# One written list of steps for attention and early routing, in place of a planner with priorities

## The chip, the cores and the metric

The program runs on one core of a Trainium2 chip. Its engines work side by side and each takes its own instructions strictly in order: TensorE (PE: matmuls and transposes into the eight PSUM banks; PEld: its weight loads), VectorE (DVE), ScalarE (ACT), GpSimd (POOL) and SyncE (SP), which only queues DMA transfers here. An instruction that waits for another engine holds up all that stands behind it on its own. The metric is the time of the whole program on the device in microseconds (us).

## What is computed

Three layers follow each other: windowed attention, a mixture of 8 experts that sends each token to one expert, and a dense layer.

```python
def _attn_ref(q, k, v):                       # (2, 8, 576, 64) each
    scores = scale * np.matmul(q, k.transpose(0, 1, 3, 2))
    mask = (rel >= 0) & (rel < 64)            # rel = row - column
    scores = np.where(mask, scores, -1000000000.0)
    attn = np.exp(scores - np.max(scores, axis=-1, keepdims=True))
    attn = attn / (np.sum(attn, axis=-1, keepdims=True) + 1e-09)
    return np.matmul(attn, v)
...
x = attn_out.transpose(0, 2, 1, 3).reshape(1152, 512)
# experts: the best of 8 by x @ w_gate, at most 288 tokens each;
# each token gets gate * (relu(x @ w1[e]) @ w2[e])    w1 (8, 512, 1024), w2 (8, 1024, 512)
# dense: h = x @ w_in; out = (h * clip(h + 3, 0, 6) / 6) @ w_out      w_in (512, 2048)
```

## The kernel before, in words

Attention goes over the 1152 tokens in nine tiles of 128 tokens with all 8 heads (j = 0 to 8); a tile has two groups g = 2j and 2j + 1. All is in float32. The steps of tile j, by the short names that the kernel gives them:

- `lq`, `lk`, `lv`: SP queues the loads of 256 KB each (L472). A load needs a free slot among 3 for q, 4 for k, 3 for v.
- `tq`, `tk`, `tv`: TensorE turns them, four transposes each (L504); `eq`, `ek`, `ev` copy the result out of PSUM, on ScalarE or VectorE (L456 to L462). `cv0`, `cv1`, `cv2` are GpSimd's copies of the values into three rotating pairs of value tiles (L486); they need the values step of three (`cv2`: two) tiles ago to be over, since it reads the tile that they overwrite. A slot for v is free when its turn and its copies are done.
- `gw`, `ew`, `tw`, `ex`: the router's product with the values (L534), its copy, a small turn (L548), and copies into columns beside the values.
- `s`: the scores of both groups, 32 small matmuls (L568). It uses one pair of banks, so the next tile's must wait until this tile's masks have read them.
- `m`: VectorE's mask with the row maximum, four pieces a group (L581). `e`: ScalarE's exponentials, four a group (L594). `pt`, `ep`: the probabilities are turned (L604) and copied out.
- `av`: the values step, 32 matmuls (L622), into the one pair of accumulator banks. `f`: VectorE's finish, which divides, adds up the router's logits (L634 to L650) and frees these banks. `st`: SP stores the tile's rows to memory (L654). In the last tile ScalarE does the division (L642).

After five tiles early routing starts: `top` chooses the expert of 640 tokens (L130 to L138), `pp` counts on TensorE, `pl`, `fl` and `gE` on VectorE pick the busiest expert and the places of its first 128 tokens, `ix` and `ie` make an index of it, and `ga` on GpSimd gathers their rows from memory by an indirect DMA (L799), `sE` scales them, `tE` turns them (L814) and `xE` copies them. `wl.u.h` are eight loads of 512 KB of that expert's weights, possible once `pl` has told which expert (L271, L274), and `e0` to `e3`, `er`, `et`, `eh` are its products for three of four units of weights. Behind the last tile `ch`, `cn`, `pL`, `rk`, `sa`, `px`, `sx` place the remaining tokens and `g0` gathers the first rows; `gt`, `hot`, `gc`, `pg`, `sg` make the gates. The rest of the experts and the dense layer follow in an order that another planner in the kernel sets; it takes over the clocks of this stage.

Each step is a node with engines and estimated costs, needs, a ring that it takes a slot of, and rings that it frees. In the kernel before, `run_nodes` (L425) plans greedily: of all nodes whose needs are met it takes the one with the smallest key, made of the time at which it could start on an engine by the planner's clocks, a priority from a table and its cost. For a copy that either engine can do, the same key picks ScalarE (A) or VectorE (V). The central lines:

```python
key = (t + EPS * prio + (c if len(engs) > 1 else min(engs.values())) * CW, prio)
able.append((key, name, e, t, c))
...
best = min(able)
```

Of the kernel before, what the change touches and what calls it, by code (L numbers as in the profile page):

```python
# [23 lines left out]
def tile_kernel(ctx, tc, q, k, v, w_gate, w1, w2, w_in, w_out, out, cap):  # L24
# [24 lines left out]
    NA = 3 * E  # L49
# [267 lines left out]
    GAP = -0.2  # L317
    EPS, CW, COLD, LAG = 0.015, 0.3, 6.0, 0.15
    PRIO = {'q': -30, 'k': -29, 'v': -27, 'tq': -7, 'eq': 8, 'tk': -10, 'ek': 3, 'cv': 1, 'tv': 1, 'ev': 2, 'gw': 1, 'ew': 1, 'tw': 1, 'ex': -4, 's': 2, 'm': 5, 'e': 2, 'pt': 2, 'ep': 9, 'av': 2, 'f': 8, 'st': 0, 'top': -5, 'tail': 2, 'ear': 78, 'hot': 60, 'gt': 25, 'fl': 13, 'ga': 58, 'xE': 5, 'turn': 20}
    CS = {'xE': 1.15, 'ep': 1.07, 'eq': 1.07, 'sE': 1.15, 'rk': 1.3, 'q': 1.15, 'v': 0.7}  # L320
    with ExitStack() as actx:
# [74 lines left out]
        nodes, done, emitted = {}, {}, []  # L396
# [3 lines left out]
        clock = dict.fromkeys(("PE", "A", "V", "P", "D"), 0.0)  # L400

        def node(name, prio, engs, fn, needs=(), take=None, free=(), lag=LAG):
            engs = {e: c * CS.get(name[0] if isinstance(name, tuple) else name, 1.0) for e, c in engs.items()}
            nodes[name] = (prio, engs, fn, needs, take, free, lag)

        def ready(name):
            _, _, _, needs, take, _, _ = nodes[name]
            r = 0.0
            for n in needs:
                if n not in done:  # L410
                    return None
                r = max(r, done[n])
            if take:
                order = taken[take]
                if len(order) >= rings[take]:
                    old = order[len(order) - rings[take]]
                    if freed.get((take, old), (0, 0.0))[0] < holders.get((take, old), 1):
                        return None
                    r = max(r, freed[take, old][1])
            return r  # L420

        holders, now = {}, [0.0]

        def run_nodes():
            while nodes:  # L425
                able = []
                for name, (prio, engs, *_) in nodes.items():
                    r = ready(name)
                    if r is None:
                        continue  # L430
                    for e, c in engs.items():
                        t = max(clock[e], r)
                        if e == "PE" and t < COLD:
                            c = 2 * c
                        key = (t + EPS * prio + (c if len(engs) > 1 else min(engs.values())) * CW, prio)
                        able.append((key, name, e, t, c))
                best = min(able)

                able = [a for a in able if a[3] + a[4] <= best[3] + GAP]
                best = min([best] + able, key=lambda a: (a is best, a[0][1])) if able else best  # L440
                _, name, e, t, c = best
                _, _, fn, _, take, free, lag = nodes.pop(name)
                if take:
                    taken[take].append(name)
                now[0] = t
                fn(e)
                clock[e] = t + c
                done[name] = t + c + lag
                for ring, owner in free:
                    n, was = freed.get((ring, owner), (0, 0.0))  # L450
                    freed[ring, owner] = n + 1, max(was, t + c + 0.1)
# [210 lines left out]
        node("wg", 6, {"D": 0.3}, lambda e: load_wg(), lag=2.0)  # L662
        node("rc", 30, {"P": 6.0}, lambda e: routing_constants())
        A_V = {"A": 0.5, "V": 0.6}
        for j in range(NJ):
            p = 10 * j + (PRIO["tail"] if j == NJ - 1 else 0)
            for nm in ("q", "k", "v"):
                node(("l" + nm, j), p + PRIO[nm], {"D": 1.25}, load_rows(nm, j), take=nm, lag=2.0)
            parts = 3 if j + 1 < NJ else 2
            holders["v", ("lv", j)] = 1 + parts  # L670
            node(("tq", j), p + PRIO["tq"], {"PE": 0.44}, turn_rows(("q", j), ("tq", j)), [("lq", j)], "t", [("q", ("lq", j))])
            node(("eq", j), p + PRIO["eq"], {"A": 0.5, "V": 0.6}, q_out(j), [("tq", j)], "qd", [("t", ("tq", j))])
            node(("tk", j), p + PRIO["tk"], {"PE": 0.44}, turn_rows(("k", j), ("tk", j)), [("lk", j)], "t", [("k", ("lk", j))])
            node(("ek", j), p + PRIO["ek"], A_V, k_out(j), [("tk", j)], None, [("t", ("tk", j))])
            for i in range(parts):
                old = j - NV + (i == 2)
                node(
                    (f"cv{i}", j), p + PRIO["cv"] + i, {"P": 0.6}, v_copy(j, i), [("lv", j)] + [("av", old)] * (old >= 0),
                    None, [("v", ("lv", j))],
                )  # L680
            node(("tv", j), p + PRIO["tv"], {"PE": 0.44}, turn_rows(("v", j), ("tv", j)), [("lv", j)], "t", [("v", ("lv", j))])
            node(("ev", j), p + PRIO["ev"], A_V, v_out(j), [("tv", j)], "vT", [("t", ("tv", j))])
            node(("gw", j), p + PRIO["gw"], {"PE": 0.27}, v_gate(j), [("ev", j), "wg"], "x", [("vT", ("ev", j))])
# [1410 lines left out]
```

## Time and profile before

| | us |
|---|---|
| median of 3 runs | 417.3 (416.82 to 417.35) |
| the profiled execution | 416.61 |
| its span, first to last instruction | 414.9 |
| TensorE busy | 400.3 (96% of the span) |
| VectorE busy | 280.1 (68%) |
| ScalarE busy | 233.9 (56%) |
| GpSimd busy | 49.3 (12%) |

Times in the trace are microseconds from the span's start. The span is shorter than the execution by what lies around it. Attention and early routing end at about 61 us; the matmuls behind them, at L244, hold the rest. Busy time of TensorE contains the latency of a matmul, so a step's price is read from its start to the next one's start.

### The profile page before, as it was taken

What the parts mean: (1) busy time and instruction counts of PE and PEld (TensorE: products, weight loads), DVE (VectorE), ACT (ScalarE), POOL (GpSimd) and SP (SyncE); (2) the same over time, 40 slices, a digit from 0 to 9 for tenths busy, and PEclk for the clock granted to TensorE, in tenths of its full rate; (3) what the DMA queues carried; (4) which work ended last, traced back from release to release, by engine and by line L of the source; (5) the groups of instructions that cost most, each with busy time, mean ns of one, the idle gap of its engine ahead of it and who ended that gap; (6) DMA issues with size and microseconds to landing.
All of it is one profiled execution on the core that took longest, in us unless ns stands there. A gap on an engine that the chain in (4) does not pass through costs nothing.

```text
span 414.9 us, 8440 instructions
## 1 busy us (share of the span) xinstructions
PE 400.3 (96%) x3066; PEld 341.7 (82%) x3066; DVE 280.1 (68%) x781; ACT 233.9 (56%) x510; POOL 49.3 (12%) x109
## 2 busy tenths in 40 slices
PE   8999889999999999999999999999999999999992
PEld 5787666668999898898989999888888888999981
DVE  1988977599789789876789999358895222322430
ACT  3886863687586747666885566267573222322330
POOL 8733402030012000000000000000000000200111
PEclk9999999999999999999999999999999999999997
DMA  9999685987787999899700560033500000100101
GB/s 168 212 217 222 218 294 171 308 285 240 228 263 226 352 300 303 286 344 346 263 2 0 165 242 0 2 101 103 203 2 2 0 0 2 74 27 2 51 28 57
DMA packets 63842, 65.43 MB, mean 158 GB/s; under 512 B 30688, under 2 KB 47072, under 8 KB 63792
## 3 DMA queue, kind: packets, MB, share of 16 engines
q1 hardware_dynamic: 62224, 59.79, 46.4%
q0 software_dynamic: 1568, 5.01, 3.6%
q8 instruction: 26, 0.43, 0.4%
q14 instruction: 24, 0.20, 0.1%
HBM read 60.08 MB, written 4.72 MB: 156 GB/s over the span
## 4 chain that ended last, share of the span: by engine, by line
PE 90%; DVE 5%; ACT 2%; issue 1%; POOL 0%; POOLq 0%; ACTq 0%; DVEq 0%
PE banks L244 76%; PE banks L504 2%; PE banks L622 2%; PE banks L568 1%; PE banks L604 1%; DVE neg L581 1%; PE banks L1475 1%; PE banks L661 1%; PE banks L1500 1%; PE banks L534 1%; PE banks L1310 1%; ACT pe L594 1%; PE banks L1559 1%; PE banks L1408 0%; DVE xt L649 0%
## 5 line engine op out<-in xcount | busy, mean ns | idle before, releaser
L244 PE MATMUL banks<-x,wt 128*128 128x320 f32 (+3 forms) x432 | 79.8, 336 | 0.0
L244 PEld LDWEIGHTS banks<-x,wt 128*128 128x128 f32 x432 | 70.8, 188 | 7.1
L244 PE MATMUL banks<-wt,g 128*128 128x512 f32 x288 | 69.6, 390 | 0.0
L263 DVE TENSOR_TENSOR wt<-raw,wt 128x512 fp32r<-128x512 f32 x100 | 64.6, 685 | 4.9 <-ACT wt L258 4.6
L1621 DVE SCALAR_TENSOR_TENSOR gf<-r,banks 128x320 f32<-128x320 f32 (+3 forms) x48 | 26.6, 553 | 60.3 <-ACT r L1618 60.1
L1618 ACT ACTIVATE r<-banks,c_three 128x320 f32<-128x320 f32 (+3 forms) x48 | 27.9, 582 | 68.4 <-PE banks L244 68.2
L244 PEld LDWEIGHTS banks<-wt,g 128*128 128x128 f32 x288 | 53.7, 188 | 10.6
L258 ACT CAST wt<-raw 128x512 fp32r<-128x512 f32 x100 | 58.7, 628 | 4.5 <-PE banks L244 4.0
L244 PE MATMUL banks<-xT,wt 128*128 128x224 f32 (+2 forms) x288 | 38.2, 282 | 0.0
L244 PE MATMUL banks<-h,wt 128*128 128x224 f32 (+2 forms) x288 | 37.0, 279 | 0.0
L244 PEld LDWEIGHTS banks<-xT,wt 128*128 128x128 f32 x288 | 34.8, 191 | 1.6 <-issue 0.4
L244 PEld LDWEIGHTS banks<-h,wt 128*128 128x128 f32 x288 | 34.6, 192 | 0.8 <-issue 0.8
L1624 ACT CAST g<-gf 128x320 fp32r<-128x320 f32 (+2 forms) x40 | 21.3, 534 | 16.4 <-DVE gf L1621 16.4
L1627 DVE TENSOR_TENSOR g<-gf,g 128x320 fp32r<-128x320 f32 (+2 forms) x40 | 23.3, 584 | 10.1 <-ACT g L1624 9.4
L1664 POOL DMA_INDIRECT out_dram<-raw,cidx x4 | 3.9, 981 | 204.5 <-DVE raw L1658 196.9
L244 PE MATMUL banks<-x,wt_fixed 128*128 128x320 f32 (+3 forms) x144 | 26.8, 337 | 0.4 <-ACT x L1391 0.4
L244 PEld LDWEIGHTS banks<-x,wt_fixed 128*128 128x128 f32 x144 | 23.5, 188 | 3.0 <-ACT x L1391 0.7
L206 ACT ACTIVATE c<-raw 128x512 f32<-128x512 f32 x32 | 21.5, 673 | 6.2 <-DVE raw L229 4.7
L244 PE MATMUL banks<-wt_fixed,g 128*128 128x512 f32 x96 | 23.2, 390 | 0.0
L222 DVE SCALAR_TENSOR_TENSOR c<-raw,c 128x512 uint32<-128x512 uint32 x32 | 22.1, 690 | 0.8
L581 DVE CUSTOM_DVE_ANT_0 neg<-banks,tmask 128x128 f32<-128x128 f32 x72 | 16.2, 286 | 9.4 <-PE banks L568 9.4
L594 ACT ACTIVATE pe<-neg,nmx 128x128 f32<-128x128 f32 x72 | 22.3, 392 | 0.1
(310 smaller groups left out, 629.4 us busy)
## 6 DMA issues: line engine op xcount, KB each, us to landing
raw<-in_moe_w_dram SPq DMA_DIRECT2D x56, 512.0 KB, 5.9
raw<-in_moe_w_in_dram SPq DMA_DIRECT2D x16, 512.0 KB, 6.6
raw<-in_moe_w_out_dram SPq DMA_DIRECT2D x16, 512.0 KB, 6.1
early<-in_moe_w_dram SPq DMA_DIRECT2D x8, 512.0 KB, 6.6
x_dram<-xt SPq DMA_DIRECT2D x9, 256.0 KB, 2.8
q_sb<-in_q_dram SPq DMA_DIRECT2D x8, 256.0 KB, 3.9
k_sb<-in_k_dram SPq DMA_DIRECT2D x8, 256.0 KB, 4.8
v_sb<-in_v_dram SPq DMA_DIRECT2D x8, 256.0 KB, 4.5
```

The source lines that it names most:

```text
L206: nc.scalar.activation(box["c"].bitcast(F32), box["hi"].bitcast(F32), AF.Abs)
L222: nc.vector.scalar_tensor_tensor(out=box["c"], in0=box["hi"], scalar=0xC0000000, in1=box["c"], op0=ALU.bitwise_and, op1=ALU.bitwise_or,)
L244: nc.tensor.matmul(out, l, r, start=(start and n == 0), stop=(stop and n == len(pairs) - 1))
L258: nc.scalar.copy(hi, r)
L263: V.tensor_tensor(out=lo, in0=r, in1=hi.bitcast(F32), op=ALU.subtract)
L504: nc.tensor.transpose(pt[:, hp, :], t[:, 2 * hp : 2 * hp + 2, :].rearrange("p h d -> p (h d)"), ident)
L581: V.tensor_tensor_reduce(out=neg[:, hp, :], in0=box["sp", g][:, hp, :], in1=tmask[:, first, :], scale=-1.0, scalar=3.0e38, op0=ALU.add, op ...
L594: nc.scalar.activation(pe[:, hp, :], neg[:, hp, :], AF.Exp, bias=nmx[:, hp : hp + 1], scale=-1.0)
L1618: nc.scalar.activation(r, ph, AF.Relu, bias=c_three)
L1621: V.scalar_tensor_tensor(out=gf, in0=r, scalar=6.0, in1=ph, op0=ALU.min, op1=ALU.mult)
L1624: nc.scalar.copy(hi, gf)
L1627: V.tensor_tensor(out=lo, in0=gf, in1=hi.bitcast(F32), op=ALU.subtract)
```

## The change

The table of priorities, the key and the choice among ready nodes go away. In their place stands a written list of all steps, `ATTENTION`, each with the engine for a copy (`:a` ScalarE, `:v` VectorE). `run_nodes` goes through it and issues step by step; each engine gets its steps in the order of the list. The clocks that it still keeps serve the planner of what follows. They start at other values, and the estimated costs of the nodes are other numbers.

```diff
+    ATTENTION = """
+        lq.0 tq.0 lk.0 tk.0 lk.1 eq.0:a lq.1 lq.2 ek.0:a tk.1 s.0 lv.0 m.0 tq.1 ek.1:a tq.2 eq.1:a m.1 e.0 wg tv.0
...
-        clock = dict.fromkeys(("PE", "A", "V", "P", "D"), 0.0)
+        clock = {"PE": 5.0, "A": 1.3, "V": 1.2, "P": 7.1, "D": 2.9}
...
         def run_nodes():
-            while nodes:
-                able = []
...
-                best = min(able)
...
+            name_of = {n if isinstance(n, str) else ".".join(map(str, n)): n for n in nodes}
+            for word in ATTENTION.split():
+                word, _, e = word.partition(":")
+                name = name_of.pop(word)
+                engs, fn, _, take, free, lag = nodes[name]
+                e = {"a": "A", "v": "V"}[e] if e else next(iter(engs))
+                t, c = max(clock[e], ready(name)), engs[e]
+                if e == "PE":
+                    if t < 7.1:
+                        c *= 1.95
+                    f = FORMS.get(word.split(".")[0], 128)
+                    if f != form[0]:
+                        form[0] = f
+                        c += 0.094
                 if take:
                     taken[take].append(name)
                 now[0] = t
                 fn(e)
                 clock[e] = t + c
-                done[name] = t + c + lag
+                done[name] = t + c + (LAG[e] if lag is None else lag)
...
-        node("ga", p + PRIO["ga"], {"P": 1.04}, early_gather, ["ie"], lag=6.0)
+        node("ga", {"P": 0.4}, early_gather, ["ie"], lag=6.0)
```

No instruction is added or taken away in sum; some copies change engine (of the copies of turned probabilities, 12 on ScalarE and 6 on VectorE, which was 14 and 4; of the other full copies more are on ScalarE). The loads stand in the order q0, k0, k1, q1, q2, v0, router weights, k2, v1 and so on, where before each tile had q, k, v in turn. TensorE's row has s.5 and s.6 ahead of the values step of tile 4; behind the routing counts stand the turn tv.5 and, further on, the last turns. On SP the load of tile 7's values stands behind those of tile 8 and needs the slot of tile 5's; behind it come the stores of tiles 4, 2, 3, 1, then six early weight loads, the store of tile 5 and two more. In the tail TensorE has pt.15, av.6, gw.8, pt.14, pt.17, tw.8, av.7, pt.16, tE between the last scores and the last values; before it had pt.15, av.7, pt.16, pt.17, tE. Behind attention it starts with three half products of the early expert before the counts, where it had two.

Three places, first as they were and then as they are (the new file's lines are a few numbers off: L655 is the old L649). VectorE from tile 3's finish on, before (`xt` and `logits` end a finish, `kT`, `vw`, `qd` are copies out of PSUM, `top_m` is the choice of experts):

```order
L650 TENSOR_REDUCE logits<-lv 128x8
L456 COPY kT<-banks 128x4x2x64
L456 COPY vw<-banks 128x128
L458 TENSOR_SCALAR qd_183<-banks 128x512
L634 TENSOR_SCALAR rd<-banks 128x8
L635 RECIPROCAL rd<-rd 128x8
L637 TENSOR_TENSOR lv<-banks,rd 128x64
L649 TENSOR_TENSOR xt<-banks,rd 128x512
L650 TENSOR_REDUCE logits<-lv 128x8
L130 TENSOR_REDUCE top_m<-logits 128x5
```

And now, from the copies ahead of tile 3's finish to the first mask piece behind it:

```order
L462 COPY pT<-banks 128x512
L462 COPY vw<-banks 128x128
L640 TENSOR_SCALAR rd<-banks 128x8
L641 RECIPROCAL rd<-rd 128x8
L643 TENSOR_TENSOR lv<-banks,rd 128x64
L655 TENSOR_TENSOR xt<-banks,rd 128x512
L656 TENSOR_REDUCE logits<-lv 128x8
L587 ISA neg,nmx<-banks,tmask 128x128
L587 ISA nmx 128x1
```

Three more pieces of this mask group follow, then the finish of tile 4 and the choice of experts. A mask group has moved ahead of the choice; two more moved ahead of it further up.

ScalarE's end of attention, before (`c` is the scaling of the gathered rows, `early` the copy of their turn):

```order
L460 COPY pT<-banks 128x512
L594 ACTIVATE pe<-neg,nmx 128x128 x8
L462 ACTIVATE c_1188<-c_1188,sgE 128x512
L460 COPY pT<-banks 128x512
L460 COPY early<-banks 128x512
```

And now:

```order
L600 ACTIVATE pe<-neg,nmx 128x128 x4
L466 COPY vw<-banks 128x128
L466 COPY pT<-banks 128x512
L600 ACTIVATE pe<-neg,nmx 128x128 x4
L466 COPY vx_187<-banks 128x8x8
L466 COPY vy_190<-banks 64x8x8
L468 ACTIVATE c_1191<-c_1191,sgE 128x512
L466 COPY pT<-banks 128x512
L466 COPY early<-banks 128x512
```

A small copy, a copy of probabilities and two pieces of router columns have come in between.

GpSimd around the gather, before (`vx`, `vy` are the value tiles, `A1t` products for the late routing, `c` the gathered rows):

```order
L486 TENSOR_SCALAR vy_189<-v_sb 64x8x64
L486 TENSOR_SCALAR vy_190<-v_sb 64x8x64
L486 TENSOR_SCALAR vx_187<-v_sb 128x8x64
L486 TENSOR_SCALAR vy_190<-v_sb 64x8x64
L891 TENSOR_TENSOR A1t<-A_93,c_tok 128x128 x5
L799 DMA c_1188<-x_dram,eI 128x512
```

And now:

```order
L492 TENSOR_SCALAR vx_186<-v_sb 128x8x64
L492 TENSOR_SCALAR vy_189<-v_sb 64x8x64
L492 TENSOR_SCALAR vx_187<-v_sb 128x8x64
L492 TENSOR_SCALAR vy_190<-v_sb 64x8x64
L800 DMA c_1191<-x_dram,eI 128x512
L892 TENSOR_TENSOR A1t<-A_93,c_tok 128x128 x2
L492 TENSOR_SCALAR vy_190<-v_sb 64x8x64
L892 TENSOR_TENSOR A1t<-A_93,c_tok 128x128 x3
```

The gather has moved ahead of the five products and of one value copy (of tile 7); the four copies in front of it are two of tile 7 and two of tile 8.

## Rows read from the trace of the kernel before

**Rows 1.** Page, chain that ended last: share of the span by engine
```profile
PE 90%; DVE 5%; ACT 2%; issue 1%; POOL 0%; POOLq 0%; ACTq 0%; DVEq 0%
```

**Rows 2.** Windows: us, PE, PEld, DVE, ACT, POOL busy, PEclk, DMA share, GB/s
```profile
20.00:25.00 5.00, 5.00 (x92) 4.03 (x91) 4.20 (x25) 4.01 (x12) 1.39 (x3) 1.00 0.81 193
...
40.00:45.00 5.00, 4.05 (x64) 2.97 (x60) 5.00 (x50) 4.66 (x15) 0.23 (x1) 1.00 0.34 74
...
50.00:55.00 5.00, 3.81 (x81) 2.84 (x79) 4.73 (x27) 3.84 (x12) 2.22 (x4) 1.00 1.07 379
```

**Rows 3.** Timeline of TensorE, one period: start us, us, instruction
```profile
21.56 0.65 PE L604 MATMUL banks<-ident,pe 128*128 128x128 f32 x4
...
23.02 1.10 PE L568 MATMUL banks<-kT,qd 64*64 64x128 f32 x32
24.06 0.66 PE L604 MATMUL banks<-ident,pe 128*128 128x128 f32 x4
24.64 0.43 PE L534 MATMUL banks<-vT,wgb 128*32 128x128 f32 x8
...
25.74 0.28 PE L622 MATMUL banks<-vy,pT 128*64 128x73 f32 x1
...
26.92 0.66 PE L604 MATMUL banks<-ident,pe 128*128 128x128 f32 x4
```

**Rows 4.** Timeline of VectorE, from the choice of experts to the last mask
```profile
38.40 0.20 DVE L130 TENSOR_REDUCE top_m<-logits 128x5 f32<-128x40 f32 x1
...
46.91 0.16 DVE L778 CAST rhsE<-et 128x5 f16<-128x5 f32 x1
...
47.38 0.60 DVE L783 TENSOR_SCALAR rhsE<-et 128x5 f16<-128x5 f32 x1
...
49.44 0.15 DVE L634 TENSOR_SCALAR rd<-banks 128x8 f32<-128x8 f32 x1
...
50.78 0.28 DVE L581 CUSTOM_DVE_ANT_0 neg<-banks,tmask 128x128 f32<-128x128 f32 x1
...
52.25 0.29 DVE L581 CUSTOM_DVE_ANT_0 neg<-banks,tmask 128x128 f32<-128x128 f32 x1
...
56.41 0.28 DVE L581 CUSTOM_DVE_ANT_0 neg<-banks,tmask 128x128 f32<-128x128 f32 x1
```

**Rows 5.** Chain in order of time, end of attention: start us, us, what
```profile
56.27 2.45 ACT pe L594 x8
58.71 0.62 ACT c L462
...
60.04 1.20 PE banks L622 x32
```

**Rows 6.** Timeline behind attention: TensorE's longest wait, the first late gather
```profile
66.69 1.13 PE L244 MATMUL banks<-early 128*128 128x256 f32 x4 [0.75 <-ACT first_w L842]
...
68.75 0.94 POOL L799 DMA_INDIRECT first_w<-x_dram,sidx  x1 [16.35 <-DVE sidx L999]
```

**Rows 7.** Page, DMA issues: tile, count, KB each, median us to landing
```profile
v_sb<-in_v_dram SPq DMA_DIRECT2D x8, 256.0 KB, 4.5
```

**Rows 8.** Groups by line, 0 to 62 us: busy us, mean ns of one
```profile
L460 ACT COPY pT<-banks 128x512 f32<-128x512 f32 x14 | 8.1, 582 | 5.4 <-PE banks L604 5.1 <-DVE nmx L581 0.3
...
L456 DVE COPY pT<-banks 128x512 f32<-128x512 f32 x4 | 2.7, 684 | 0.0
...
L456 DVE COPY vw<-banks 128x128 f32<-128x128 f32 x6 | 1.7, 290 | 0.5 <-PE banks L534 0.4
```

**Rows 9.** Timeline of GpSimd before the early gather
```profile
47.29 0.65 POOL L486 TENSOR_SCALAR vy<-v_sb 64x512 f32<-64x512 f32 x1 [7.07 <-PE banks L622]
...
51.21 1.20 POOL L799 DMA_INDIRECT c<-x_dram,eI  x1 [0.18 <-DVE nmx L581]
```

**Rows 10.** Tiles c (the early gather) and early (its expert's weights): from issue to landing
```profile
DMA to landing us min/median/max: 7.1/7.1/7.1
...
DMA to landing us min/median/max: 3.5/6.6/8.2
```

More of the change, by code (lines that the diff above doesn't have):

```diff
@@ L399, in tile_kernel, with node @@
         freed = {}
-        clock = dict.fromkeys(("PE", "A", "V", "P", "D"), 0.0)
-        def node(name, prio, engs, fn, needs=(), take=None, free=(), lag=LAG):
-            engs = {e: c * CS.get(name[0] if isinstance(name, tuple) else name, 1.0) for e, c in engs.items()}
-            nodes[name] = (prio, engs, fn, needs, take, free, lag)
+        clock = {"PE": 5.0, "A": 1.3, "V": 1.2, "P": 7.1, "D": 2.9}
+        def node(name, engs, fn, needs=(), take=None, free=(), lag=None):
+            nodes[name] = (engs, fn, needs, take, free, lag)
         def ready(name):
-            _, _, _, needs, take, _, _ = nodes[name]
+            _, _, needs, take, _, _ = nodes[name]
             r = 0.0
             for n in needs:
-                if n not in done:
-                    return None
                 r = max(r, done[n])
@@ L415, in ready @@
                 if len(order) >= rings[take]:
[L416 to L419, printed above, removed]
-            return r
-        holders, now = {}, [0.0]
+                    r = max(r, freed[take, order[len(order) - rings[take]]])
+            return r
+        now, form = [0.0], [128]
+        FORMS = {"gw": 32, "s": 64, "av": 73}
+        LAG = {"PE": 0.2, "V": 0.14, "A": 0.15, "P": 0.1, "D": 1.5}
         def run_nodes():
-            while nodes:
-                able = []
[L427 to L436, printed above, removed]
-                best = min(able)
[L439 to L442, printed above, removed]
+            name_of = {n if isinstance(n, str) else ".".join(map(str, n)): n for n in nodes}
[12 more added lines that the diff above has]
+                        c += 0.094
                 if take:
@@ L677, in tile_kernel @@
                 node(
[L678 removed]
+                    (f"cv{i}", j), {"P": 0.6}, v_copy(j, i), [("lv", j)] + [("av", old)] * (old >= 0),
                     None, [("v", ("lv", j))],
                 )
[L681 to L682 removed]
@@ L702, in tile_kernel @@
                 needs += [("ex", j - 1), ("cv2", j - 1)]
[L703 removed]
+            node(("av", j), {"PE": 1.1}, values(j), needs, "o", free)
             if j + 1 < NJ:
[L705 to L711 removed]
+                node(("f", j), {"V": 1.35}, lambda e, j=j: finish(j), [("av", j)], "xt", [("o", ("av", j))])
+                node(("st", j), {"D": 0.75}, lambda e, j=j: store_x(j), [("f", j)], None, [("xt", ("f", j))])
+            else:
+                node(("f", j), {"V": 1.0}, lambda e, j=j: finish(j), [("av", j)])
         A1E = ac.tile([128, NE, 128], F16, name="A1E")
```

138 lines of the change are left out of this document (70 added, 68 removed).

## The prediction, made before the changed kernel ran

> **What bounds the kernel now.** I read the chain of waits first: 90% of the span is TensorE, so the kernel as a whole is bound by the matrix engine, and VectorE has 5% [rows 1]. Next the windows of five microseconds, to see where TensorE is short of work: it is busy 5.00 of 5.00 us from 20 to 25, but 4.05 from 40 to 45, 3.81 from 50 to 55 [rows 2]. So attention falls in two parts. In the first, the timeline of TensorE shows a period of 5.36 us for a tile of 128 tokens (the same transposes start at 21.56 and at 26.92) with nothing idle between; a new order can gain nothing there, it can only lose. In that period a score step (L568) takes 1.04 us, a router step, a turn and the small turn behind it 1.10 together, and the 32 matmuls with the values 1.18 [rows 3]. In the second part VectorE is the limit: it is busy 5.00 of 5.00 us from 40 to 45 and 4.73 from 50 to 55 [rows 2]. There it has the early routing between the mask steps: from the choice of experts at 38.40 until the last mask (56.41 + 0.28 = 56.70) it works with hardly a gap for 18.3 us [rows 4]. The last piece is ScalarE's: the chain goes from the masks to eight exponentials (56.27 to 58.71), the scaling of the gathered rows, the turn of these and, at 60.04, the last matmuls with the values [rows 5]. Whatever brings these forward brings everything behind them forward, since TensorE has little idle time after it: the largest left is 0.75 us at 66.69 [rows 6].
>
> **The change part by part.** I sum from one event to the next, in the profiled execution's own time (416.61 us, of which 414.9 are the span; 0.7 below the median of 417.30). The difference is then taken from the median.
>
> *Up to the finish of tile 4.* The new row of TensorE has, before the values step of tile 4, two score steps more and one v turn, one router step and one small turn less: 2 x 1.04 - 1.10 = +1.0 us [rows 3]. Its kinds of steps are the same and the number of changes between them nearly so, so while TensorE is full, the finish of tile 4 comes 1.0 us later: VectorE's choice of experts starts at 38.40 + 1.0 = 39.4. The start of the kernel bounds this from both sides. The new load order asks for tile 0's values sixth instead of third, and a load of values takes 4.5 us from issue to landing [rows 7], several under way at once; a turn that waits for one may wait about a microsecond (an estimate: the period of 5.36 us covers three loads and a store, so a load each 1.2 us or so). Against that, fewer turns wait there for a ScalarE copy. I take 0, with +-1.0 for the range.
>
> *VectorE from the choice to the last mask.* The order shows the same instructions there except for these, which the new order leaves out of the stretch: three mask groups of four pieces, now ahead of tile 4's finish; one finish of a tile, now behind the masks; two copies of turned probabilities and one small router copy, now on ScalarE. Prices: eight mask pieces start from 50.78 to 52.25, 0.21 each, so 12 x 0.21 = 2.5; a finish from 49.44 to 50.78, 1.3; the copies 2 x 0.68 + 0.29 = 1.65, of which the end overlaps the next instruction, so 1.5 [rows 4, 8]. Together 5.3 us of 18.3; 13.0 stay. The last mask ends at 39.4 + 13.0 = 52.4 instead of 56.7. The one before it ends 0.84 sooner, at 51.6.
>
> *ScalarE's tail.* What went off VectorE comes back here, and this is the cost of the change. Behind the masks the old row has two exponential steps (2.45), the scaling (0.62) and one copy. The new row has: exponentials 1.22, a small copy 0.29, a copy 0.58, exponentials 1.22, two pieces of the router columns (0.4, an estimate from the 0.29 of the small copy, which VectorE needs), the scaling 0.62, a copy 0.58, and about 0.2 until the matmuls start [rows 5, 8]: 5.1 us. From 51.6 that ends at 56.7. But a copy stands ahead of these exponentials that needs a turn which TensorE does behind the last score step; I put 0.6 for that, which makes 57.3. A second way to the same matmuls agrees: the accumulator bank. Tile 6's finish follows the last mask (52.4 + 1.3 = 53.7), then tile 7's values (1.18, + 0.3 for two hand-overs), then its finish 1.3 and 0.2: 56.7 if nothing else is late. I take 57.3 against 60.0 before: **-2.7 us**.
>
> *The gather.* On GpSimd it now stands behind four value copies, two of them of tile 7. That tile's load is queued on the load queue behind one that needs tile 4's value step, and its slot comes free with a turn that stands behind the routing counts. Step by step: choice 39.4 + 1.3, counts and turn 1.0 (41.7), load 4.5 (46.2), four copies at 0.65 (48.8), gather 7.1 from issue to landing (55.9) [rows 7, 9, 10]. From landing to the last values the new ScalarE row has scaling 0.62 and copy 0.58, with hand-overs 1.4: 57.3. It is just hidden, and bounds the end as much as ScalarE does. Before, it landed at 51.21 + 7.1 = 58.3, just under the exponentials that ended at 58.7, so it hid there too. Bounds by the nearest rows: the weight loads beside it landed in 3.5 to 8.2 us [rows 10], so 3.6 less, which the other two ways hide, or 1.1 more. The early weights are asked for behind that load and four stores, from about 43.5 on. The first one used is the fifth in the row; asked for some 2 us later, it is there by 54 even at 8.2, before it is needed: nothing gained or lost.
>
> *Behind attention.* The order of what follows is nearly the same. The counts for the late routing come after one more half product (about +0.9 us for VectorE's ranks), and TensorE's wait of 0.75 at 66.69 [rows 6] gets work beside it. VectorE has slack there, and all weights are asked for from the same points of the chain. I take 0, bounds -0.7 and +0.9.
>
> Sum: -2.7 us; 416.6 would become 413.9, and the median 417.3 becomes **414.6 us**.
>
> **A rule weighed.** The last routing step L783, 5 elements a row, took 0.60 us where its like L778 took 0.16; it ended at 47.98, just behind a value copy of GpSimd that ran from 47.29 to 47.94 [rows 4, 9]. The Trainium skill (SBUF — State Buffer, "SBUF: two separate sides") says that VectorE, in an instruction with two SBUF inputs or in a two-port mode, and GpSimd share a port pair as an exclusive lock, so that the loser waits for the whole instruction. By that rule, with which the trace agrees, this change can cost what rival (a) does; without it the sum stands.
>
> **The rivals.** (a) *Vector steps held by GpSimd's copies.* Before, GpSimd stood idle for 7.07 us while VectorE did the routing [rows 9], so only one copy met it. Now value copies run while the gate step is under way or just behind. If all four hold a step as the one above was held (0.45 us), VectorE's stretch grows by 1.8 us and the gain shrinks to 0.9: 416.4. For it: the row. Against: most vector steps there read PSUM or are over in 0.2 us, and all four would have to meet one. (b) *More than forecast.* The waits in the tail fall away, and TensorE is left with its own work: its idle time is 0.95 us from 40 to 45 and 1.19 from 50 to 55 [rows 2], and the chain shows TensorE out of 2.4 us while the eight exponentials run. All of it gone is 4.5 us: 412.8. Against: one accumulator bank pair and ScalarE's longer tail. (c) *Slower: the gather becomes the bound.* Behind the counts the row is serial: turn, load of tile 7's values, copies, gather, scaling, copy. It decides once the gather lands later than about 58.6, that is, when load and gather together take over 14.3 us instead of 11.6. With tile 7's load as slow as the slowest weight load, 8.2 us [rows 10], the gather lands at 41.7 + 8.2 + 2.6 + 7.1 = 59.6 and the last values start at 61.0: +1.0, 418.3. For it: TensorE's row has the turn of the gathered rows ahead of the last values, so nothing slips past it. Against: the weight loads are queued behind this load, and the gather's 7.1 was measured with them under way. (d) *The kernel's rest takes the gain back*, because the weight stream and not TensorE sets the pace behind attention: 417.2. Against it stand the chain's 90% on TensorE [rows 1] and that the loads are asked for from the same chain.
>
> **How the numbers follow.** Forecast 0.56, its own range 413.2 to 416.0 from the +-1.0 of the start and the two ends of the last part. (a) 0.14, (b) 0.14, (c) 0.10, (d) 0.06. A measurement of this kernel tells 0.2%, 0.8 us, from no change. Faster: forecast, (b), and most of (a): 0.56 + 0.14 + 0.10 = 0.80. The same: the rest of (a), (d) less a bit: 0.09. Slower: (c) and a lost start: 0.11. The range reaches into (b) below and to where (d) and the mild half of (c) lie above: 412.4 to 417.6.
>
> **What would show it.** In the new profile: TensorE full up to about 36 us; the choice of experts (L130) within 1 us of 39.4; the last mask near 52.4 with no copy of probabilities on VectorE between; ScalarE nearly without a gap from there to the last values; the gather issued near 48.8 and landed before 56; the last values near 57.3; the first gather behind attention 2 to 3 us sooner than 68.75 [rows 6]. The prediction is wrong if TensorE waits at the start for loads by more than a microsecond, if the gather is issued after 51, or if the last values come sooner and the kernel ends no sooner.

## The result, and the profile after

The changed kernel takes **413.25 us** (median of 4 runs, 412.68 to 413.33) against 417.13 us for the kernel before on the same chip (4 runs, 416.82 to 417.35): ratio 0.9905, 95% interval 0.9887 to 0.9922, so 3.9 us or 0.9% faster. Forecast were 414.6 us, with a range of 412.4 to 417.6 and a chance of 0.80 for faster. The profiled span went from 414.9 to 411.5 us, but TensorE's last matmuls start 3.92 us earlier (402.42, now 398.50): behind the last matmul, where the output is written, the second profile takes half a microsecond longer.

The chain of waits in the new profile, shares by engine, answers to [rows 1]. VectorE went from 5% to 3%, and DMA, which had no share before, now has 3%:

```profile
PE 89%; DMA 3%; DVE 3%; ACT 2%; issue 1%; POOL 0%; POOLq 0%; ACTq 0%; DVEq 0%
```

The windows answer to [rows 2] (same columns, with two more windows):

```profile
20.00:25.00 5.00, 5.00 (x94) 4.34 (x94) 4.79 (x27) 4.48 (x14) 2.44 (x4) 1.00 1.00 194
40.00:45.00 5.00, 4.84 (x88) 3.85 (x87) 5.00 (x42) 4.59 (x15) 1.20 (x2) 1.00 0.86 253
45.00:50.00 5.00, 4.14 (x74) 3.02 (x69) 4.88 (x34) 4.94 (x16) 3.21 (x5) 1.00 0.96 339
50.00:55.00 5.00, 4.82 (x89) 3.98 (x87) 4.05 (x25) 4.52 (x16) 0.00 (x0) 1.00 1.08 368
55.00:60.00 5.00, 3.88 (x47) 3.30 (x46) 2.62 (x11) 2.90 (x9) 1.73 (x4) 1.00 0.93 340
```

From 40 to 45 TensorE has 4.84 us of work instead of 4.05, from 50 to 55 it has 4.82 instead of 3.81. VectorE is still nearly full from 40 to 50 (5.00 and 4.88); ScalarE now is too, up to 55 (4.59, 4.94 and 4.52). What is left idle on TensorE lies mostly from 45 to 50 (0.86 us) and from 55 to 60 (1.12).

VectorE's timeline answers to [rows 4] (start, us, engine, line, operation):

```profile
35.73 0.29 DVE L587 CUSTOM_DVE_ANT_0 neg<-banks,tmask 128x128 f32<-128x128 f32 x1 [0.27 <-PE banks L574]
...
38.43 0.20 DVE L130 TENSOR_REDUCE top_m<-logits 128x5 f32<-128x40 f32 x1
...
41.46 0.58 DVE L745 TENSOR_SCALAR nsub<-subE 128x8 bf16<-128x8 f32 x1
...
42.01 0.63 DVE L756 TENSOR_TENSOR top_f<-oh,subE 128x40 f32<-128x40 bf16 x1
...
45.60 0.60 DVE L784 TENSOR_SCALAR rhsE<-et 128x5 f16<-128x5 f32 x1
...
46.94 0.15 DVE L793 CAST eI<-banks 128x1 int32<-128x1 f32 x1
...
51.54 0.28 DVE L587 CUSTOM_DVE_ANT_0 neg<-banks,tmask 128x128 f32<-128x128 f32 x1
```

One mask group starts at 35.73, ahead of the choice of experts (L130), which starts at 38.43 as it did before (38.40). The index is cast at 46.94 (in [rows 4] the finish right behind the index started at 49.44), and the last mask piece ends at 51.82 instead of 56.70. Three tiny steps of the routing take about 0.6 us each where their likes take 0.15 to 0.19.

The chain in front of the last values answers to [rows 5] (start, us, what was on it), and GpSimd's timeline to [rows 9]:

```profile
47.38 8.07 DMA c<-x_dram,eI
...
55.48 0.73 ACT c L468
...
56.25 0.66 PE banks L815 x4
56.91 1.11 PE banks L628 x29
```

```profile
47.38 1.19 POOL L800 DMA_INDIRECT c<-x_dram,eI  x1 [0.64 <-DVE sgE L795]
```

The gather of the early rows is issued at 47.38 instead of 51.21, right behind the index and its scale (L795 ends at 47.34), and is on the chain with its whole 8.07 us: ScalarE's scaling waits for it, and the last values start at 56.84, 3.1 us sooner than before. TensorE's timeline, for [rows 3] and [rows 6]:

```profile
22.30 0.28 PE L628 MATMUL banks<-vy,pT 128*64 128x73 f32 x1
...
23.48 0.42 PE L540 MATMUL banks<-vT,wgb 128*32 128x128 f32 x8
23.84 1.10 PE L574 MATMUL banks<-kT,qd 64*64 64x128 f32 x32
24.87 0.66 PE L610 MATMUL banks<-ident,pe 128*128 128x128 f32 x4
25.37 1.04 PE L510 MATMUL banks<-ident,v_sb 128*128 128x128 f32 x8
26.24 0.27 PE L554 MATMUL banks<-ident,vw 128*128 128x128 f32 x1
26.35 0.62 PE L610 MATMUL banks<-ident,pe 128*128 128x128 f32 x4
26.81 0.60 PE L510 MATMUL banks<-ident,k_sb 128*128 128x128 f32 x4
27.24 0.60 PE L510 MATMUL banks<-ident,q_sb 128*128 128x128 f32 x4
27.68 0.62 PE L610 MATMUL banks<-ident,pe 128*128 128x128 f32 x4
28.23 0.28 PE L628 MATMUL banks<-vy,pT 128*64 128x73 f32 x1
...
62.77 0.44 PE L854 MATMUL banks<-ident,first_w 128*128 128x128 f32 x2 [0.26 <-DMA x_dram<-xt]
...
70.87 0.60 PE L1961 MATMUL banks<-ident,first_w 128*128 128x128 f32 x4
```

In the first part the router step (L540) now stands right ahead of the score step (L574), and the turns stand together; the lines run from the values of tile 1 (22.30) to those of tile 2 (28.23). Behind attention the wait of 0.75 us at 66.69 [rows 6] is gone, 0.26 is left at 62.77, and the turn of the remaining rows (L1961) starts at 70.87 where it started at 74.81: 3.94 us sooner, 3.1 of them from the last values and 0.8 from there on.

### The profile page after: what moved, and what is told of

It is laid out like the page before. It is cut to its first block, busy times and chain, and to the rows that moved or that the text cites. A ratio compares the mean times of both kernels' runs of the same rounds, so it can differ in the third digit from the quotient of the medians.

```text
span 411.5 us, 8431 instructions
## 1 busy us (share of the span) xinstructions
PE 398.0 (97%) x3066; PEld 341.2 (83%) x3066; DVE 277.5 (67%) x772; ACT 236.0 (57%) x519; POOL 49.7 (12%) x109
## 4 chain that ended last, share of the span: by engine, by line
PE 89%; DMA 3%; DVE 3%; ACT 2%; issue 1%; POOL 0%; POOLq 0%; ACTq 0%; DVEq 0%
PE banks L244 75%; PE banks L510 2%; DMA c<-x_dram,eI 2%; PE banks L574 2%; PE banks L628 2%; PE banks L610 1%; PE banks L1473 1%; PE banks L667 1%; PE banks L1498 1%; DMA out_dram<-part,cidx 1%; PE banks L1308 1%; PE banks L1557 1%; DMA x_dram<-xt 1%; PE banks L1406 0%; PE banks L540 0%
```

## The experiments

The theory to test: the last values come 3.1 us sooner since VectorE's stretch between the choice of experts and the index is shorter (a mask ahead of the choice, copies on ScalarE), the first part does more work in the same time since TensorE changes the shape of its matmuls less often, and 0.8 us come from the order behind attention. The gather bounds the last values now. Rivals are named at each run. Every kernel below is the changed one with another list (or the lines shown); the planner of the experts behind the list gets the clock readings that it has in the changed kernel, so that everything behind the list is the same.

**Two halves.** The new list up to the choice with the old order behind it, and the reverse.

```diff
 # new_to_choice
-<the changed list>
+<the changed list up to top> <the rest in the old order, ep.12 ep.14 ew.8 on VectorE, hotp.0 to hotp.4 ahead of ga>
 # old_to_choice
+<the old order up to top> m.11 s.6 ... <the rest in the changed list's order>
```

> The changed list up to the choice of experts (the first stretch, with masks 10 to 12 already ahead of the choice), and behind it the old order with the old engines: VectorE gets back two pT copies and a vw copy, and the one-hot products stand ahead of the gather on GpSimd. First theory (the gain lies in VectorE's stretch, half of it ahead of the choice and half in the copies that went to ScalarE): the choice starts at 38.4 us as in the changed kernel, the index is ready about 0.6 us later, at 48, the last mask comes at 54 to 55 instead of 51.8, so ScalarE's last exponentials end at 57 and the last values start at about 58.5 instead of 56.9; with the waits behind attention back (0.8), the time is about 415.5 us. Rival (all of the gain is made in the first stretch, by fewer changes of the matmul's shape): last values at 57, time about 413.5 to 414.

> The old order up to the choice of experts, and behind it the changed list: masks 10 to 13 stand behind the choice and ahead of the places, the copies go to ScalarE as in the changed kernel. First theory (masks in the chain from choice to index are what cost): the choice at 38.4, the index three masks of 1.0 us later than in the changed kernel, 50.2 instead of 47.2, the gather lands 8 us behind it, last values at 59 to 60, time about 416. Rival (what is done ahead of the choice doesn't matter, only the copies on ScalarE and the loads behind): last values at 57, time about 413.3.

Measured: 418.26 us, ratio 1.0037 (1.0023 to 1.0051), and 419.27 us, ratio 1.0059 (1.0044 to 1.0074). Both halves are slower than the kernel before, and both theories missed. VectorE's timeline shows why, first of the one, then of the other:

```profile
40.21 0.29 DVE L462 COPY vw<-banks 128x128 f32<-128x128 f32 x1 [0.89 <-PE banks L540]
42.84 0.17 DVE L734 SCALAR_TENSOR_TENSOR e<-banks,c_desc 128x8 f32<-128x8 f32 x1 [2.33 <-ACT qd L468]
```

```profile
42.67 0.29 DVE L587 CUSTOM_DVE_ANT_0 neg<-banks,tmask 128x128 f32<-128x128 f32 x1 [1.30 <-PE banks L574]
...
46.21 0.17 DVE L734 SCALAR_TENSOR_TENSOR e<-banks,c_desc 128x8 f32<-128x8 f32 x1 [1.77 <-PE banks L729]
```

The first step of the places (L734) comes 2.4 and 5.8 us later than in the changed kernel (40.40). TensorE's counts (L729), which it reads, end just before it, at 42.73 and 46.11 (in the first the trace names a ScalarE copy, which ends at 42.78). TensorE's queue is in order, and the counts stand behind steps that the other half has not fed in time: in the first behind waits of 0.68, 0.48, 0.65 and 0.38 us, in the second behind scores that waited 2.57 us for a mask. What stands ahead of the choice is right here only with what stands behind it. The two runs say nothing on where the gain is; the next ones change one thing each.

**One mask behind the choice.**

```diff
-... m.12 ek.7:a pt.10 ... f.4 top gw.6
+... ek.7:a pt.10 ... f.4 top m.12 gw.6
```

> The changed list with one mask, group 12, moved from ahead of the choice of experts to right behind it. In the changed kernel's trace this mask runs at 35.73 to 36.65 us, while VectorE would wait for the values of tile 4 anyway. Theory (a mask that runs in that wait is free, and one that stands between the choice and the index delays the gather by its 0.85 us, with what waits for its scores): the choice at 38.2 as before, the index and the gather 0.85 us later, at 48.2, and since the gather bounds the last values, these start at 57.6 to 57.7: time about 414.1. Rival 1 (VectorE is not what sets the index; the chain waits for TensorE's counts in any case): gather at 47.4, time 413.3. Rival 2 (what waits for that mask's scores' place, the scores of tile 7 and the steps behind them on TensorE's queue, delays the counts as well): index 1.5 us or more later, time 415 or more.

Measured: 414.03 us, ratio 0.9931 (0.9911 to 0.9951); 0.8 us of the gain are gone by the medians, as the theory said, though the two intervals overlap. In its profile the choice is at 38.41, the gather at 48.55, 1.2 us later, and the last values at 58.48, 1.6 later. Of the gather's 1.2 us the mask makes 0.8 (the first step of the places, L734, starts at 41.22 instead of 40.40) and longer holds 0.3: four steps instead of three are held for a while, where like ones take 0.16 to 0.25 us. GpSimd's copies run from 41.56 to 42.77 and from 45.76 to 47.00 (lines below). Behind the gather comes this execution's clock: TensorE waited 1.16 us for the routing at 47.41, and from 50 to 53 its granted clock was 0.53 (near the lower level) where the changed kernel has 1.00, so ScalarE came later too.

```profile
41.67 0.55 DVE L739 TENSOR_SCALAR e<-e,e 128x8 f32<-128x8 f32 x1
...
42.25 0.54 DVE L741 TENSOR_TENSOR subE<-e,e 128x8 f32<-128x8 f32 x1
...
45.84 0.60 DVE L779 CAST rhsE<-et 128x5 f16<-128x5 f32 x1
46.34 0.71 DVE L159 TENSOR_SCALAR A<-c_i128h,sb 128x128 f16<-128x128 f16 x1
```

**GpSimd's copies behind the gather.**

```diff
-... cv0.7 ... cv1.7 ... cv0.8 ... cv1.8 ... ga hotp.3
+... ga cv0.7 cv1.7 cv0.8 cv1.8 hotp.3
```

> The changed list, with GpSimd's four copies of v for tiles 7 and 8 moved behind the early gather. First theory (VectorE steps of the chain from choice to index are held by GpSimd's copies, three times, 1.35 us in all): the three steps last 0.1 to 0.2 us instead of 0.6, the gather is issued at about 46.0 instead of 47.4 and lands 8 us later at 54.1, and the last values start at about 56.0, now bound by ScalarE's last exponential (54.6) as well: time about 412.4. First rival (the gather lands when the weight loads issued ahead of it are done, whenever it is issued): issued at 46.0 but landing at 55.5, time 413.3. Second rival (the holds move to the masks behind the index, and the values of tile 7 wait for the late copies): last values at 57.5 or later, time 413.9 or more.

Measured: 412.75 us, ratio 0.9896 (0.9882 to 0.9910). VectorE's timeline, the same three steps and the index:

```profile
41.33 0.16 DVE L745 TENSOR_SCALAR nsub<-subE 128x8 bf16<-128x8 f32 x1
...
41.52 0.19 DVE L756 TENSOR_TENSOR top_f<-oh,subE 128x40 f32<-128x40 bf16 x1
...
44.67 0.17 DVE L784 TENSOR_SCALAR rhsE<-et 128x5 f16<-128x5 f32 x1
...
46.07 0.16 DVE L793 CAST eI<-banks 128x1 int32<-128x1 f32 x1 [0.40 <-PE banks L789]
```

The holds are gone: 0.16, 0.19 and 0.17 us instead of 0.58, 0.63 and 0.60, and from the first step of the places (L734) to the index it is 5.80 us (40.27 to 46.07) instead of 6.54 (40.40 to 46.94). So GpSimd's copies did hold VectorE, the mechanism of rival (a). Three of the four copies met a step and held it, 1.3 us together; 0.74 of this reached the index, since without the holds VectorE waits 0.40 us for TensorE in front of it. How many steps are met changes from profile to profile: old_behind, copies_back and loads_last (below) have the same steps in this stretch and GpSimd's copies in it, but two shorter holds (L756 and L750), and the index is 5.99 to 6.03 us behind L734, only 0.2 more than here. (The Trainium skill, SBUF — State Buffer, "SBUF: two separate sides", says that at the pair of ports which the two share the engine that comes second waits for the whole instruction of the other; the trace agrees: the three steps end at 42.04, 42.64 and 46.20, and the copies that they met at 42.01, 42.60 and 46.17.) But the gather was issued only 0.26 us sooner, at 47.12, 0.9 behind its index instead of 0.3, and the last values came 0.4 us sooner (56.43). Why GpSimd took 0.6 us longer to start is open; the two later runs with this edit have the same 0.9.

**What the gather waits for.** Loads of the early experts' weights moved behind it, all eight or five of them.

```diff
-... wl.2.1 ... wl.3.1 ... wl.0.0 ... wl.2.0 ... wl.1.0 ... ga ... wl.1.1 ... st.5 wl.0.1 wl.3.0
 # loads_last
+... ga ... st.5 ... st.7 wl.0.0 wl.1.0 wl.2.0 wl.0.1 wl.1.1 wl.2.1 wl.3.0 wl.3.1
 # loads_three_first
+... wl.0.0 wl.1.0 wl.2.0 ... ga ... st.5 wl.0.1 wl.1.1 wl.2.1 wl.3.0 wl.3.1
```

> The changed list with all eight loads of the early experts' weights (512 KB each) put behind the store that follows the values of tile 7, at about 56 us, so that nothing but the store of tile 5 stands in the DMA queues beside the gather. A measurement of the disputed time by itself. Theory (the gather's 8.1 us from issue to landing are mostly waiting behind the six loads issued ahead of it): it lands 3 to 4.5 us behind its issue, at 50.5 to 52, and ScalarE's exponentials bound the last values, at about 56.0; the early experts then wait for their weights, first product at 60 or later, time 415 to 418. Rival (the 8 us belong to the gather itself, row by row): it lands at 55.4 as before, last values 56.9, time 416 to 419.

> The changed list with only three of the early experts' loads (the first halves, which the first products need) ahead of the gather and five behind the store of tile 5. Theory (the gather waits behind the loads ahead of it): with three loads instead of six it lands 5 to 6.5 us behind its issue, at 52.5 to 54, the last values start at 56.0 to 56.3, bound by ScalarE, and the loads behind are still in time for the second halves (from 64 us): time about 412.5. Rival 1 (loads issued behind the gather share the DMA engines with it just as well): landing at 55.4, time 413.3. Rival 2 (the five later loads come too late for the early experts or push the next weights back): last values 56.2, but TensorE waits behind attention, time 414 or more.

Measured: 421.22 us, ratio 1.0103 (1.0088 to 1.0117), and **412.09 us, ratio 0.9879 (0.9865 to 0.9893)**. The gather's issue and its median us to landing, with three loads of 512 KB issued ahead and with none (8.07 in the changed kernel, with six):

```profile
c<-x_dram,eI POOLq DMA_INDIRECT x1, 6.1
```

```profile
c<-x_dram,eI POOLq DMA_INDIRECT x1, 3.7
```

So 4.4 of the 8.1 us go away with the loads. But the number ahead is not all. The two runs that follow have the same three loads ahead, first loads_and_copies, then two_more_to_vector:

```profile
c<-x_dram,eI POOLq DMA_INDIRECT x1, 6.7
```

```profile
c<-x_dram,eI POOLq DMA_INDIRECT x1, 4.2
```

What differs is how soon the store of tile 5, with the next loads behind it, follows the gather: 1.4 us where it took 6.7 (47.03 and 48.44), 2.0 where it took 6.1 (47.19 and 49.18), 3.1 where it took 4.2 (47.41 and 50.51). So transfers issued behind the gather seem to slow it as well, as rival 1 had it; no run changes this alone. With three ahead it lands before ScalarE is ready: ScalarE's scaling starts at 54.25 with no wait, right behind the last exponentials and two small copies, and the last values start at 55.77, 1.07 sooner; the later loads are still in time. With none ahead the last values start at 55.62, hardly sooner, but TensorE then waits 7.10 us for weights, and the first twelve products take 4.79 us instead of 2.86: the granted clock was 0.64 from 60 to 64, where TensorE waited, and 0.51 from 64 to 68.

**Both repairs, and a step further.**

```diff
 # loads_and_copies: the edits of copies_later and loads_three_first
 # two_more_to_vector: the same, and
-... ep.12:a ... ep.17:v pt.16 ex.8:a f.7 sE:a
+... ep.12:v ... ep.17:v sE:v pt.16 ex.8:a f.7
```

> The changed list with both repairs: three early loads ahead of the gather and five behind the store of tile 5, and GpSimd's four copies for tiles 7 and 8 behind the gather. With three loads ahead the gather had landed at 53.4 and ScalarE, busy without a gap from 41 to 55.5 us, bounded the last values at 55.77. Theory (ScalarE is now the bound): the index is ready 0.8 us earlier and the gather lands by 53, but the last values start at 55.6 to 55.8: time 412.0. Rival (the gains add, because VectorE's earlier masks let ScalarE start its exponentials earlier): last values at 55.3, time 411.6.

> As with both repairs, and two of ScalarE's steps given to VectorE: the copy of pT group 12 (0.58 us, right behind the index) and the scaling of the gathered rows (0.72 us on ScalarE). Theory (ScalarE's uninterrupted work from 41 us bounds the last values, and VectorE has the 0.8 us that the copies no longer hold): the last exponentials end 0.5 us earlier, the last values start at 55.1 to 55.3, time about 411.5. Rival (VectorE waits for the gather in front of the finish of tile 7, or its masks come later by what it was given): last values at 55.8 or later, time 412.1 or more.

Measured: 412.31 us, ratio 0.9883 (0.9867 to 0.9900), last values at 55.77, the same to a hundredth as with the loads alone: ScalarE is the bound then. And 412.87 us, ratio 0.9894 (0.9877 to 0.9910), last values at 56.97, as the rival had it. VectorE waits in front of the copy for TensorE's turn, and the masks behind it in its queue wait too; the last mask piece starts at 52.67 instead of 51.20 in loads_and_copies:

```profile
47.78 0.69 DVE L462 COPY pT<-banks 128x512 f32<-128x512 f32 x1 [1.01 <-PE banks L610]
...
52.67 0.29 DVE L587 CUSTOM_DVE_ANT_0 neg<-banks,tmask 128x128 f32<-128x128 f32 x1
```

**The copies back to VectorE**, on the changed kernel as it is.

```diff
-ep.12:a ... ew.8:a ... ep.14:a
+ep.12:v ... ew.8:v ... ep.14:v
```

> The changed list with the copies of pT groups 12 and 14 and of vw tile 8 given back from ScalarE to VectorE, at the same places in the order. VectorE gets 1.66 us more work behind the index, ScalarE 1.4 us less. Theory (the early gather now bounds the last values, with 0.9 us to spare for the rest): the last mask comes at 53.4 instead of 51.8, ScalarE's last exponentials end at 56.0, so the scaling of the gathered rows starts about 0.5 us later and the last values at 57.3 to 57.4: time about 413.7. Rival 1 (VectorE is still what bounds): last values 1.66 later, 58.5, time 414.9. Rival 2 (ScalarE was the nearest bound, so relieving it pays for the later masks): last values at 56.9, time 413.3.

Measured: 413.52 us, ratio 0.9922 (0.9909 to 0.9935): 0.3 us slower than the changed kernel, too little to tell from its interval. In the profile the last values start at 57.51, 0.7 later, near what the theory gave, but by another way: the last mask is only 0.7 later (52.53) and the gather, issued at 46.73 in this execution, had landed by 53.95. ScalarE waits 2.02 us for a turn of probabilities (from 54.67, the end of its scaling, to 56.69), which stands on TensorE behind the values of tile 7; these start at 54.82 instead of 53.30, since one of the copies that they need now stands on VectorE behind a finish. Giving these copies to ScalarE is worth 0.7 us at the last values of one profile; in the medians the 0.3 us are within the noise.

**Shapes of matmuls.** Two attempts to put changes of shape back, both with the same work.

```diff
 # more_shapes
-... lk.4 ... av.0 ... gw.1 ... s.3 ... pt.3 ... tw.1 ... tv.2 tk.4 ... gw.2 ... s.4 ... tv.4 ... gw.3 ... s.5 ... tk.6
+... tk.3 lk.4 ... av.0 tk.4 ... s.3 ... pt.3 gw.1 ... tv.2 tw.1 ... s.4 ... tv.4 gw.2 ... s.5 ... tk.6 gw.3
 # shapes_mixed: in the score step of tiles 3 to 5
 for hp in range(H // 2):
+    if j in (3, 4, 5):
+        nc.tensor.matmul(<gate product hp of tile j - 2, which v_gate no longer issues>)
     ...
```

> The changed list with the gate products of tiles 1 to 3 (32-column weights) taken out from between the values and the scores and put between two 128-column steps, and one key turn put between the values and the scores of tile 3: TensorE changes the shape of its matmuls 29 times up to the values of tile 4 instead of 25; the same work otherwise. Theory (a change of shape costs TensorE about 0.14 us, and the first stretch gained 1.0 us by having fewer): values of tile 4 start 0.4 to 0.6 us later than 35.63, the choice at 38.9 to 39.0 instead of 38.4, last values 57.4, time about 413.8. Rival (the first stretch gained by something else, and a change of shape costs nothing): values of tile 4 at 35.6, time 413.3.

> The changed kernel, with the four gate products (32-column weights) of tiles 1 to 3 each issued ahead of a quarter of the score step that follows them, instead of all four ahead of it: the same instructions, in the same steps, with 18 more changes of the matmul's shape up to the choice of experts, and no other step moved. The earlier attempt moved a key turn, which then waited 1.65 us, so it told nothing of shapes. Theory (a change costs TensorE 0.09 to 0.15 us, and the first stretch gained by having fewer of them): the mixed score steps take 0.5 to 0.9 us longer each, the choice starts 1.6 to 2.7 us later, at 39.8 to 40.9 instead of 38.2, and the time is 414.5 to 416. Rival (changes of shape cost nothing; the first stretch gained by other steps): the choice at 38.2, time 413.3.

The first: 418.02 us, ratio 1.0030 (1.0016 to 1.0044), choice at 43.05. It doesn't tell, since the moved key turn made TensorE's next turn wait 1.65 us for ScalarE and more steps wait behind it. The second: 417.32 us, ratio 1.0008 (0.9997 to 1.0018). TensorE's timeline around the first mixed step:

```profile
18.42 0.41 PE L573 MATMUL banks<-vT,wgb 128*32 128x128 f32 x2
18.76 0.45 PE L579 MATMUL banks<-kT,qd 64*64 64x128 f32 x8
19.14 0.41 PE L573 MATMUL banks<-vT,wgb 128*32 128x128 f32 x2
...
20.90 0.45 PE L579 MATMUL banks<-kT,qd 64*64 64x128 f32 x8
21.28 0.66 PE L615 MATMUL banks<-ident,pe 128*128 128x128 f32 x4
```

From 18.42 to 21.28 the mixed step takes 2.86 us, where the same 40 matmuls of the trace take 1.39 in the changed kernel (23.48 to 24.87 above). One gate product alone takes 0.34, four in a row 0.36; a quarter of the scores takes 0.38, all four 1.03. So nearly all of a short step's time is paid once for each run of one shape: about 0.33 us for the gate's, 0.16 for the scores' ((4 x 0.38 - 1.03) / 3). With 18 changes more the choice starts at 42.98 instead of 38.43, 4.6 us later or 0.25 each, and the whole gain of the changed kernel is gone. (The Trainium skill, TensorEngine Tiling (Array Packing), "Tiling Modes", says that a change of tiling mode drains TensorE; the trace agrees that each change costs time, 0.25 us here. How much of it is the drain no run separates.)

**The part behind attention.**

```diff
-av.8 f.8 e0.1 ch e1.1 e0.0 pL er.1:v ...
+av.8 hotp.1 hotp.2 hotp.4 f.8 e0.0 ch e1.0 cn pL er.0:a ... <the old order to its end>
```

> The changed list up to the last values, and behind them the old order of the early experts and the late routing. Theory (the part behind attention gave 0.8 us, two TensorE waits of 0.75 and 0.15 us that are gone): last values at 56.9 as in the changed kernel, the waits back, the rest's turn 14.8 us behind the last values as in the kernel before instead of 14.0, time about 414.1. Rival (those waits went because attention ended earlier in relation to the loads, not by the order): the turn stays 14.0 us behind, time 413.3.

Measured: 413.73 us, ratio 0.9931 (0.9914 to 0.9949). TensorE's timeline:

```profile
62.84 1.13 PE L244 MATMUL banks<-early 128*128 128x256 f32 x4 [0.75 <-ACT first_w L843]
...
71.02 0.60 PE L1964 MATMUL banks<-ident,first_w 128*128 128x128 f32 x4
```

The wait of 0.75 us is back, and the remaining rows' turn starts 13.66 us behind the end of the last values (57.36), as in the kernel before (13.60, from 61.21 to 74.81), instead of 12.79 in the changed one (58.08 to 70.87): 0.87 us, the theory's term. The median is only 0.5 us longer, within the intervals, and the profiled execution (413.18 us) is no longer than the changed kernel's (413.24): its gather was issued 0.6 sooner, at 46.77, with two holds of VectorE in front instead of three, and its last values start at 56.12.

## Why the prediction was right, and where it was not

The sign and the mechanism of the second part held; the time came out 1.3 us below the forecast, at the lower edge of its own range (413.2 to 416.0).

| step | forecast | measured |
|---|---|---|
| choice of experts starts | 39.4 | 38.43 |
| choice to end of last mask | 13.0 | 13.4 (13.3 without GpSimd's holds, in copies_later) |
| last mask ends | 52.4 | 51.82 |
| gather issued, landed | 48.8, 55.9 | 47.38, 55.45 |
| last values start | 57.3 (-2.7) | 56.84 (-3.1) |
| behind attention | 0 | -0.8 |

- *Up to the finish of tile 4.* The step that failed is the sentence that the number of changes of shape was "nearly" the same, and with it that TensorE, being full, can gain nothing. Up to the values of tile 4 the old order has 30 changes and the new one 25. The period of [rows 3], 5.36 us for five long turns, a router step with its small turn, scores and values, compares with 5.93 for seven long turns and the same rest (22.30 to 28.23, where the values of tiles 1 and 2 start); less two turns at 0.435 that is 5.06, 0.3 a tile for two changes fewer. Waiting less is not the reason: TensorE is idle for 2.1 us up to 35.62 in both profiles. Five changes at 0.15 make 0.75 of the 1.0 us; the rest is open, and no run tests this stretch by itself, since more_shapes doesn't tell. Full does not mean at its fastest: a busy engine's row still holds time that another order saves. shapes_mixed shows the price of such changes, and that it can eat the whole gain.
- *VectorE's stretch.* Right in size, but in part by luck. The holds of rival (a), 1.3 us, are in the 13.4; yet without them it is 13.3 (copies_later, 38.30 to 51.57), as VectorE then waits 0.9 us for TensorE: 0.4 in front of the index and 0.5 for the last scores. So VectorE's work alone is shorter than summed, and TensorE is close behind it. mask_behind shows the term at work: one mask behind the choice puts the index 0.8 us later by itself.
- *ScalarE's tail.* Summed as the bound at 57.3, it was not: its other work ended at 54.58, 0.9 before the gather landed. It is the next bound (loads_three_first), at 55.77.
- *The gather.* "Just hidden" was wrong by little: it bounds the last values. That it landed at 55.45, near the 55.9 of the sum, is luck, as two errors offset each other. It was issued 1.4 us sooner than summed. The sum lets the load of tile 7's values wait for a turn behind the counts, until 41.7, as it takes the slot to be tile 5's; the third load of values ahead of it is tile 6's, and SP issued it at 38.30, right behind GpSimd's last copy of tile 6 (until 38.27). The four copies were done by 46.75, and the gather waited for the index. And it took 8.07 us instead of 7.1. Six weight loads stood ahead of it before, too, but the last of them was issued 4.7 us ahead of the gather (46.55), now 1.0 (46.42); that this is the reason is not tested. Rival (c) had the right place, but not its price.
- *Behind attention.* Taken as 0 with -0.7 as a bound; 0.8 to 0.9 were gained, since early products now stand where TensorE had waited for a ScalarE copy.

Last values 3.1 and the part behind 0.8 make 3.9, the measured difference; the weight stream took nothing back, as every anchor of TensorE from 71 us to its last matmul is 3.9 us earlier.

What the experiments point to is a list with only three early loads ahead of the gather: 412.09 us, 1.2 us below the changed kernel by the medians (ratios to the kernel before of 0.9879 and 0.9905, whose intervals just overlap; the last values at 55.77 instead of 56.84 say the same).

## What to carry to other kernels

When a wait is removed, look for what lands next: here the gather, which was under way for 3.7 to 8.1 us, by what else the DMA queues held around it. Count the changes of matmul shape in a row of TensorE before saying that a full engine can't gain. And test a written order by moving one step at a time; the halves of two good orders made a bad one here, twice.

## What the runs showed of the hardware

- A change of matmul shape cost TensorE 0.15 us in the ordinary order (from one tile's period of each kernel), a third of a long turn (0.44), and 0.25 us in shapes_mixed.
- A 256 KB gather by GpSimd's descriptors landed 3.7 us after its issue with no weight load ahead, 4.2 to 6.7 behind three loads of 512 KB (the longer, the sooner the next store and loads followed), and 7.1 to 8.1 behind six.
- GpSimd's copies held small VectorE steps for 0.3 to 0.5 us each, different ones from profile to profile: L745, L756 and L784 in the changed kernel, L739, L741, L779 and L159 in mask_behind, L756 and L750 in old_behind. The mask pieces beside the copy from 46.14 to 46.75 of the changed kernel were not held (0.28 us each).
- TensorE's clock fell within attention where TensorE waited. In old_to_choice it was busy 0.85 of 3 us from 38 to 41, and the two windows behind (us, PE, PEld, DVE, ACT and POOL busy, PEclk) have a granted clock of 0.79 and 0.65, between full speed and half of it:

```profile
38.00:41.00 3.00, 0.85 (x32) 0.60 (x24) 2.75 (x20) 1.74 (x6) 1.20 (x2) 1.00 0.79 184
41.00:44.00 3.00, 2.58 (x40) 2.23 (x40) 1.70 (x17) 2.01 (x6) 0.00 (x0) 0.79 0.29 97
44.00:47.00 3.00, 3.00 (x44) 2.24 (x46) 1.23 (x14) 1.88 (x6) 0.00 (x0) 0.65 0.00 0
```
